# V on ScalarE's DMA queue, K and the weights on SyncE's, in a decode attention kernel

## The chip, the cores and the metric

The kernel runs on one core of a Trainium2 chip. The time is the device time of one execution in microseconds (us); less is better. The core has five engines with their own programs: TensorE (PE, matrix products; PEld are its weight loads), VectorE (DVE), ScalarE (ACT), GpSimd (POOL) and SyncE (SP). They meet only through semaphores. DMAs are issued from an engine's program into that engine's queue, and 16 DMA engines move the data from HBM into SBUF. In the profile "SPq" and "ACTq" are rows of an engine's sequencer, such as the issue of a DMA.

## What is computed

One decode step of attention over a cache, times a gate from a small MLP. B = 2, D = 512, H = 32 heads of Dh = 128, and 8192 cached positions, all in float32:

```python
x  = A_x                                  # [2, 1, 512]
xn = layernorm(x)
q  = (xn @ wq) split into 32 heads        # [2, 32, 1, 128]
scores = q . k_cache * Dh**-0.5           # k_cache, v_cache: [2, 32, 8192, 128]
o  = softmax(scores) . v_cache
s  = o (heads joined, 4096) @ wo          # [2, 1, 512]
g  = silu(gelu(layernorm(xn) @ w1 + b1) @ w2 + b2)
return x + s * g
```

K and V have 268 MB each, wq and wo 8 MB each.

## The kernel before

The 64 heads (2 batches of 32) are taken in N = 32 pairs. A pair's K is 8.39 MB and fills one big SBUF buffer of 128 partitions with 64 KB each: the lower 64 partitions hold one head, the upper 64 the other, 128 positions a partition. There are three such buffers. KBUF[0] and KBUF[1] take K of even and odd pairs, VB takes V of every pair. K and V of pair n are called K(n) and V(n) here. VB holds w1, w2 and the small operands of the setup before V(0), and wo after the last V that it takes; KBUF[1] holds wq at first; V(31) goes into KBUF[0], in two halves.

Each engine loops over the pairs on its own.

- VectorE, `scores`: waits for K(n), multiplies it by q in place (TENSOR_TENSOR, 128x16384), sums over the head's width (TENSOR_REDUCE into sc), takes the maximum per partition (MX), and, after TensorE has transposed MX, the negative maximum per head (nm).
- TensorE, `softmax(n)`: two dummy matmuls (`unread`, bank<-Q,ident, whose result nobody reads), the transpose of MX (signals p_m), and the spread of nm over the partitions. The first of these last matmuls signals p_k: KBUF of this pair is free. The second signals p_n.
- ScalarE: bias from p_n, two exponentials into PZ (s_pz), then it waits for `weighted`, copies its sums out of PSUM (the COPY o<-bank, signal s_o4), and, after p_t, copies the pair's result into OT (a_ot).
- TensorE, `weighted(n)`: waits for s_pz and for V(n) (d_v), 32 matmuls PZ x V (bank<-big,PZ; each of these fp32 matmuls is two rows in the trace), p_v; then, after s_o4, four matmuls (bank<-mod,o). The first of them signals p_free: VB is free. The last signals p_t.

TensorE's order is softmax(0), then for each pair weighted(n), softmax(n+1), and weighted(31) at the end.

SyncE issues all large loads on one queue. Its loop takes p_k, issues K(n+2), takes p_free, issues V(n+1). `take` waits until a semaphore has a count and takes it off again. So in the queue stand K(1), V(0), K(2), V(1), K(3) and so on. At the end come K(31) in two halves, V(30), V(31) in two halves, and then, after p_free of pair 30, wo in eight pieces. ScalarE issues three small loads at the very start (x, b1 and b2, of 4, 5.4 and 2 KB), while SyncE issues w2's last rows, w1, wq, K(0) and the rest of w2.

After the loop the pieces are joined (Z, OA, rl, "on"), "on" is multiplied by wo, and the gate and x are applied.

All operations are recorded through the helper `op`, so nearly all of them have its line, L51, in the profile; L45 is `take` and L41 `wait`. The groups are told apart by the names of their tiles; "big" is any of the three buffers.

Of the kernel before, what the change touches and what calls it, by code (L numbers as in the profile page):

```python
# [4 lines left out]
AF = mybir.ActivationFunctionType  # L5
# [8 lines left out]
class Program:  # L14
# [24 lines left out]
    def wait(self, eng, *tokens):  # L39
        for name, v in self.need(eng, tokens):  # L40
            self.engines[eng].wait_ge(self.sem(name), v)  # L41

    def take(self, eng, name, v=1):

        self.engines[eng].wait_ge(self.sem(name), v).then_inc(self.sem(name), -v)  # L45

    def op(self, eng, method, *args, waits=(), sig=None, by=1, quiet=False, **kwargs):
        need = self.need(eng, waits)
        for name, v in need[:-1]:
            self.engines[eng].wait_ge(self.sem(name), v)  # L50
        ins = getattr(self.engines[eng], method)(*args, **kwargs)  # L51
        for name, v in need[-1:]:
            ins._wait_ge(self.sem(name), v)
        if quiet:
            return None
        name = sig or "own_" + eng
        by = 16 if method == "dma_start" else by
        ins.then_inc(self.sem(name), by)
        self.counts[name] += by
        return name, self.counts[name]  # L60


def decode_kernel(nc, x, kc, vc, wq, wo, w1, b1, w2, b2, out):
# [5 lines left out]
    U = 2  # L69
    HP = P // U  # L70
    KP = S // HP
    HH = H // U
    N = B * HH
    HG = 512 // DH
    NG = H // HG
    SCALE = float(DH) ** -0.5
# [4 lines left out]
    JW = 512 // DH  # L81
# [14 lines left out]
    op, wait, take = pr.op, pr.wait, pr.take  # L96

    def sb(shape, name):
        return nc.alloc_sbuf_tensor(name, list(shape), F32).ap()
# [5 lines left out]
    vf = vc.rearrange("b h s d -> (b h s d)").rearrange("(n p j d) -> n p j d", p=P, j=KP, d=DH)  # L105
# [3 lines left out]
    KBUF, VB = rows[:2], rows[2]  # L109
    used = [0]  # L110

    def boot(p, n):
        a = used[0]
        used[0] += n
        assert used[0] <= KP * DH
        return big[2][:p, a:a + n]
# [10 lines left out]
    sel = boot(P, P)  # L127
# [22 lines left out]
    th = sb([P, P], "th")  # L150
# [5 lines left out]
    SC = [sb([P, KP], f"sc{i}") for i in range(2)]  # L156
    MX = sb([P, 1], "MX")
    nm = sb([1, U], "nm")
    bias = sb([P, 1], "bias")
    RS = sb([P, N], "RS")  # L160
    PZ = sb([P, NT, U, JW], "PZ")
    o4 = sb([P, JW * DH], "o4")
    OT = sb([P, BH], "OT")
# [7 lines left out]
    po = bank[0]  # L171
    pm = bank[1]
    pn = bank[2]
    pt = bank[3]
# [13 lines left out]
    PE_EVENTS = ["xnT", "yT", "ph", "phT", "pq", "pqa"] + [f"pb{g}" for g in range(N // NPB)] + ["pg", "pgate"]  # L188

    def pe(name):  # L190
        return "pe_setup", PE_EVENTS.index(name) + 1

    def pe_n(name, n):
        return name, n + 1

    t = {}
# [9 lines left out]
    def load_k(n, *waits):  # L206
        sems, cuts = ([f"d_k{n % U}", "d_kl"], HALVES) if n == N - 1 else ([f"d_k{n % U}"], (0, KP))
        for name, (c0, c1) in zip(sems, zip(cuts, cuts[1:])):
            op("SP", "dma_start", KBUF[n % U][:, c0:c1], kf[n][:, c0:c1], sig=name, waits=waits)
# [17 lines left out]
    for k in (7, 6, 1, 2, 4, 0):  # L227
# [13 lines left out]
                  op=ALU.add)  # L241
# [59 lines left out]
                     waits=[t["x4m"]])  # L301


    wait("SP", t["sel"], t["qnat"], pe(PE_EVENTS[-1]))
    op("SP", "dma_start", VB, vf[0], sig="d_v")
    kp, vp = (a.rearrange("(i u) p j d -> i u p j d", u=U) for a in (kf, vf))
    with nc.sync.Fori(0, N // U - 2) as i:
        for u in range(U):
            take("SP", "p_k")
            op("SP", "dma_start", KBUF[u], kp[i + 1, u], sig=f"d_k{u}")  # L310
            take("SP", "p_free")
            op("SP", "dma_start", VB, vp[i, 1] if not u else vp[i + 1, 0], sig="d_v")
    for n in range(N - 2 * U, N - 2):
        take("SP", "p_k")
        load_k(n + 2)
        take("SP", "p_free")
        op("SP", "dma_start", VB, vf[n + 1], sig="d_v")
    take("SP", "p_k")
    for i, (c0, c1) in enumerate(zip(HALVES, HALVES[1:])):
        op("SP", "dma_start", KBUF[N % U][:, c0:c1], vf[N - 1][:, c0:c1], sig=f"d_v31{i}")  # L320
    take("SP", "p_free")
    wo_v = wo.rearrange("(p c) n -> p c n", p=P)
    for i, (c0, c1) in enumerate(zip(WO_CUTS, WO_CUTS[1:])):
        for h, (n0, n1) in enumerate(zip(LAST_COLS, LAST_COLS[1:]) if c1 == OC else [(0, D)]):
# [23 lines left out]
    scores(1, Q[:, N - 1, :], ["d_k1", "d_kl"], HALVES)  # L348


    with nc.scalar.Fori(0, N // U) as i:
        for u in range(U):
            take("ACT", "p_n")
            op("ACT", "copy", bias, pn[:, :1], sig="s_b")
            take("ACT", "s_b")
            sc = SC[u].rearrange("p (t j) -> p t j", j=JW)
            for s in range(U):
                r = slice(HP * s, HP * (s + 1))
                op("ACT", "activation", PZ[r, :, s, :], sc[r], AF.Exp, bias=bias[r], scale=SCALE,
                   accum_out=RS.rearrange("p (i u) -> p i u", u=U)[r, i, u:u + 1], sig="s_pz", quiet=s < U - 1)  # L360
            take("ACT", "p_v")
            op("ACT", "copy", o4, po, sig="s_o4")
            take("ACT", "p_t")
            op("ACT", "copy", OT.rearrange("p (i u s) -> p i u s", u=U, s=U)[:, i, u, :], pt[:, :U], sig="a_ot")
    t["OT"] = "a_ot", N

    t["gate"] = op("DVE", "scalar_tensor_tensor", gate, th, 1.0, z, op0=ALU.add, op1=ALU.mult,
# [9 lines left out]
                 op=ALU.mult, waits=[t["rl"], t["on0"], pe_n("p_oa", 0)])  # L377
# [33 lines left out]
    for c in range(ND):  # L411
# [4 lines left out]
        j, k = NF % QT, NF // QT  # L416
# [6 lines left out]
    j, k = NF % QT, NF // QT  # L423
    mm(ph[R * j:R * j + B, k * P:k * P + FT], ones[:1, :B], b1_sb[:, NF * P:], start=False, stop=True, sig="ph")
    by_tile = ident.rearrange("p (j r) -> p j r", r=R)
    for k in range(NH):
        n = min(QT, NF + 1 - k * QT)
# [16 lines left out]
    for g in range(N // NPB):  # L444
        mm(PB[g % len(PB)], sides, QN[:, g * NPB:(g + 1) * NPB, :].rearrange("h n d -> h (n d)"),
           waits=[t["side"], t["QN rest" if g else "QN first"]] + ([t[f"Q{QH}"]] if g >= len(PB) else []),
           sig=f"pb{g}")
    for f in range(NF + 1):
        j = f % QT
# [4 lines left out]
    for j in range(QT):  # L454
        mm(pgate[R * j:R * j + MB, :], mod_b[:, :MB], g_nat[:, j * P:(j + 1) * P], waits=[t["g"], t["mod_b"]],
           sig="pgate" if j == QT - 1 else None)
# [64 lines left out]
    for b in range(B):  # L521
        h = slice(b * H, (b + 1) * H)
        mm(OA[:, b, :OC], Z[:, h].rearrange("p h r -> p (h r)"), mod, waits=[t["Z"]],
           sig="p_oa" if b == B - 1 else None)
    unread(1)
    for i, (c0, c1) in enumerate(zip(WO_CUTS, WO_CUTS[1:])):
        for c in range(c0, c1):
            after = [t["on"], t["mem"], (f"d_wo{i}", 16)]
            if c < WIDE:
                j = c % QT  # L530
# [39 lines left out]
```

## Time and profile before

| what | value |
|---|---|
| median of 3 runs | 1300.62 us (1300.08 to 1300.69) |
| the profiled execution | 1299.61 us |
| its span in the trace | 1298.3 us |
| busy: VectorE, TensorE, ScalarE | 1135.7, 460.9, 72.0 us |
| read from HBM | 559.30 MB, 431 GB/s over the span |
| SyncE's queue (q1) | 559.30 MB, its packets 99.7% of the span of 16 DMA engines |
| ScalarE's queue (q10) | 8 packets, 0.01 MB |

The span is the stretch that the profiler recorded; the execution's own time lies 1.3 us above it. In the queue rows the share is the time that a queue's packets took, of 16 DMA engines over the span. A timeline row gives the start and the duration in us, the engine, the operation, output<-input and how many instructions were merged; in brackets stands how long the engine idled ahead of it. An issue row of a DMA ends long before the data has landed; the landing times are listed apart, as the median from issue to landing.

### The profile page before, as it was taken

The page shows a single profiled execution, that of the slowest core. Times are in us where ns is not written, and L with a number is a line of the kernel's source. Part 1 is how long each engine was busy: PE and PEld are TensorE (multiplying, and loading weights), DVE is VectorE, ACT ScalarE, POOL GpSimd, SP SyncE. Part 2 cuts the span into 40 slices and gives each one's busy share as a digit, 9 for nine tenths or more (in the row PEclk, how much of TensorE's full clock was granted, in tenths as well). Part 3 has the DMA queues.
Part 4 walks back from the last instruction along what each step waited for, and adds up shares of the span by engine and source line. Part 5 has one row for each costly group of instructions (what it writes and reads, how often), then busy time and mean ns, then how long its engine had stood idle before and what let it go on. Part 6 is the DMA issues. An engine that isn't in the chain of part 4 may idle for free. (4 is left out here: it accounts for less than half of the span.)

```text
span 1298.3 us, 7389 instructions
## 1 busy us (share of the span) xinstructions
PE 460.9 (35%) x2958; PEld 148.7 (11%) x2958; DVE 1135.7 (87%) x171; ACT 72.0 (6%) x245; POOL 2.1 (0%) x14
## 2 busy tenths in 40 slices
PE   3813433322433322343322334322334321343337
PEld 1201111001111000111100111100111100111103
DVE  2599999988889988889988888988888988888991
ACT  1100000000000000000000000000000000000000
POOL 0000000000000000000000000000000000000000
PEclk8756776567677556777656777656776666677659
DMA  9999999999999999999999999999999999999998
GB/s 410 436 428 442 430 432 432 428 444 428 438 430 428 440 428 444 428 434 430 428 444 428 440 430 426 440 428 444 428 434 430 430 442 428 440 430 430 423 436 361
DMA packets 11242, 559.39 MB, mean 431 GB/s; under 512 B 1264, under 2 KB 1536, under 8 KB 1892
## 3 DMA queue, kind: packets, MB, share of 16 engines
q1 hardware_dynamic: 11228, 559.30, 99.7%
q8 instruction: 4, 0.07, 0.0%
q10 hardware_dynamic: 8, 0.01, 0.0%
q14 instruction: 2, 0.02, 0.0%
HBM read 559.30 MB, written 0.00 MB: 431 GB/s over the span
## 5 line engine op out<-in xcount | busy, mean ns | idle before, releaser
L51 DVE TENSOR_TENSOR big<-big,Q 128x16384 f32<-128x16384 f32 (+1 forms) x33 | 551.3, 16707 | 73.2 <-DVEq L45 73.2
L51 DVE TENSOR_REDUCE sc<-big 128x128 f32<-128x16384 f32 (+1 forms) x33 | 551.2, 16703 | 4.8
L51 PE MATMUL bank<-big,PZ 128*8 128x512 f32 x2048 | 291.1, 732 | 628.9 <-PEq L45 628.9
L51 PEld LDWEIGHTS bank<-big,PZ 128*8 128x8 f32 x2048 | 60.1, 103 | 832.6 <-issue 832.6
L51 PE MATMUL bank<-Q,ident 128*128 128x512 f32 (+2 forms) x198 | 78.5, 506 | 0.2 <-issue 0.2
L51 ACT COPY o<-bank 128x512 f32<-128x512 f32 x33 | 19.4, 586 | 891.6 <-ACTq L45 880.0
L51 PE MATMUL bank<-ident,MX 128*1 128x128 f32 x32 | 9.3, 291 | 137.9 <-PEq L45 137.8
L51 PE MATMUL bank<-mod,o 128*128 128x2 f32 x256 | 32.8, 250 | 27.4 <-PEq L45 27.4
L51 PEld LDWEIGHTS bank<-mod,o 128*128 128x128 f32 x256 | 31.0, 191 | 55.4 <-issue 55.4
L51 PEld LDWEIGHTS bank<-Q,ident 128*128 128x128 f32 x198 | 33.6, 198 | 16.5 <-issue 16.5
L51 ACT ACTIVATE PZ<-sc,bias 64x128 f32<-64x128 f32 x64 | 25.5, 399 | 6.6 <-ACTq L45 6.2
L51 DVE TENSOR_REDUCE nm<-bank 1x2 f32<-1x128 f32 x32 | 8.9, 279 | 18.9 <-DVEq L45 18.9
L51 DVE TENSOR_TENSOR big<-big,mine 64x512 f32<-64x512 f32 (+1 forms) x2 | 4.5, 2279 | 21.6 <-ACT big L51 21.6
L51 PEld LDWEIGHTS bank<-ident,MX 128*1 128x1 f32 x32 | 2.5, 79 | 162.9 <-issue 162.9
L51 ACT COPY bias<-bank 128x1 f32<-128x1 f32 x32 | 5.1, 159 | 225.2 <-ACTq L45 225.2
L51 PE MATMUL bank<-nm,srow 1*64 1x1 f32 x128 | 10.4, 219 | 10.0 <-PEq L45 9.4
L51 PE MATMUL bank<-big,sides 64*128 64x512 f32 x16 | 12.6, 958 | 3.7 <-DVE big L51 3.7
L51 DVE TENSOR_REDUCE MX<-sc 128x1 f32<-128x128 f32 x32 | 9.2, 286 | 4.7
L51 PE MATMUL bank<-big,xnT 128*2 128x512 f32 x64 | 9.3, 748 | 10.3 <-DMA big<-in_A_wq_dram 10.3
L51 ACT ACTIVATION_READ_ACCUMULATOR PZ<-sc,bias x64 | 11.8, 184 | 0.0
L51 DVE SCALAR_TENSOR_TENSOR res<-bank,gate 128x128 f32<-128x128 f32 x1 | 0.3, 292 | 12.1 <-PE bank L51 12.1
L51 PEld LDWEIGHTS bank<-nm,srow 1*64 1x64 f32 x128 | 8.6, 165 | 16.2 <-issue 16.2
(78 smaller groups left out, 74.8 us busy)
## 6 DMA issues: line engine op xcount, KB each, us to landing
big<-in_A_k_cache_dram SPq DMA_DIRECT2D x2, 4096.0 KB, 35.9
big<-in_A_v_cache_dram SPq DMA_DIRECT2D x2, 4096.0 KB, 35.9
big<-in_B_w_dram SPq DMA_DIRECT2D x1, 2752.0 KB, 10.2
big<-in_B_w_dram SPq DMA_DIRECT2D x1, 2560.0 KB, 52.1
big<-in_A_wo_dram SPq DMA_DIRECT2D x1, 2560.0 KB, 14.7
big<-in_A_wo_dram SPq DMA_DIRECT2D x1, 2048.0 KB, 19.3
big<-in_A_wo_dram SPq DMA_DIRECT2D x1, 1536.0 KB, 22.5
big<-in_A_wo_dram SPq DMA_DIRECT2D x1, 1024.0 KB, 24.5
```

The source lines that it names most:

```text
L51: ins = getattr(self.engines[eng], method)(*args, **kwargs)
```

## The change

V(0) to V(30) are issued by ScalarE into ScalarE's queue. V(0) is issued after th, the last operation of ScalarE's setup. In the loop over the pairs, ScalarE takes p_free behind the copy o<-bank, issues V(n+1), and goes on to p_t and OT. SyncE's loop keeps K alone. V(31) stays on SyncE's queue, and wo there waits for a_ot of pair 30 where it took p_free before. ScalarE's last two pairs stand outside of its loop, without a load.

```diff
-    wait("SP", t["sel"], t["qnat"], pe(PE_EVENTS[-1]))
-    op("SP", "dma_start", VB, vf[0], sig="d_v")
     kp, vp = (a.rearrange("(i u) p j d -> i u p j d", u=U) for a in (kf, vf))
     with nc.sync.Fori(0, N // U - 2) as i:
         for u in range(U):
             take("SP", "p_k")
             op("SP", "dma_start", KBUF[u], kp[i + 1, u], sig=f"d_k{u}")
-            take("SP", "p_free")
-            op("SP", "dma_start", VB, vp[i, 1] if not u else vp[i + 1, 0], sig="d_v")
     for n in range(N - 2 * U, N - 2):
         take("SP", "p_k")
         load_k(n + 2)
-        take("SP", "p_free")
-        op("SP", "dma_start", VB, vf[n + 1], sig="d_v")
     take("SP", "p_k")
...
-    take("SP", "p_free")
+    wait("SP", ("a_ot", N - 1))
...
-    with nc.scalar.Fori(0, N // U) as i:
+    wait("ACT", t["sel"], t["th"])
+    op("ACT", "dma_start", VB, vf[0], sig="d_v")
+
+    def weights(u, i, following):
+        take("ACT", "p_n")
...
+        take("ACT", "p_v")
+        op("ACT", "copy", o4, po, sig="s_o4")
+        if following is not None:
+            take("ACT", "p_free")
+            op("ACT", "dma_start", VB, following, sig="d_v")
+        take("ACT", "p_t")
+        op("ACT", "copy", OT.rearrange("p (i u s) -> p i u s", u=U, s=U)[:, i, u, :], pt[:, :U], sig="a_ot")
+
+    with nc.scalar.Fori(0, N // U - 1) as i:
         for u in range(U):
...
+            weights(u, i, vp[i, 1] if not u else vp[i + 1, 0])
+    for u in range(U):
+        weights(u, N // U - 1, None)
```

SyncE's loop, two pairs, before (the row "ISA" is a `take`; in brackets is the semaphore that it waits for):

```order
L51 ISA [waits p_k]
L51 DMA big<-in_A_k_cache_dram 128x16384
L51 ISA [waits p_free]
L51 DMA big<-in_A_v_cache_dram 128x16384
L51 ISA [waits p_k]
L51 DMA big<-in_A_k_cache_dram 128x16384
L51 DMA big<-in_A_v_cache_dram 128x16384 [waits p_free]
```

The same engine from the loop's first row to the first piece of wo, in the changed kernel:

```order
L51 ISA [waits p_k]
L51 DMA big<-in_A_k_cache_dram 128x16384
L51 ISA [waits p_k]
L51 DMA big<-in_A_k_cache_dram 128x16384
L305 REGISTER_ALU
L305 COMPARE_AND_BRANCH
L51 DMA big<-in_A_k_cache_dram 128x16384 [waits p_k]
L51 DMA big<-in_A_k_cache_dram 128x8192 [waits p_k]
L51 DMA big<-in_A_k_cache_dram 128x8192
L51 DMA big<-in_A_v_cache_dram 128x8192 [waits p_k]
L51 DMA big<-in_A_v_cache_dram 128x8192
L51 DMA big<-in_A_wo_dram 128x5120 [waits a_ot]
```

V has left the loop with its wait; of V only the two halves of V(31) are still there.

ScalarE's loop, the first of its two pairs, before:

```order
L51 COPY bias<-bank 128x1 [waits p_n]
L51 ISA [waits s_b]
L51 ACTIVATE PZ,RS<-sc,bias 64x32x4
L51 ISA
L51 ACTIVATE PZ,RS<-sc,bias 64x32x4
L51 COPY o<-bank 128x512 [waits p_v]
L51 ISA [waits p_t]
L51 COPY OT<-bank 128x2
```

And in the changed kernel:

```order
L51 COPY bias<-bank 128x1 [waits p_n]
L51 ISA [waits s_b]
L51 ACTIVATE PZ,RS<-sc,bias 64x32x4
L51 ISA
L51 ACTIVATE PZ,RS<-sc,bias 64x32x4
L51 COPY o<-bank 128x512 [waits p_v]
L51 ISA [waits p_free]
L51 DMA big<-in_A_v_cache_dram 128x16384
L51 ISA [waits p_t]
L51 COPY OT<-bank 128x2
```

The wait for p_free and the issue of the next V stand between the two copies; the rest is in the order of before.

More of the change, by code (lines that the diff above doesn't have):

```diff
@@ L348, in decode_kernel @@
     scores(1, Q[:, N - 1, :], ["d_k1", "d_kl"], HALVES)
-    with nc.scalar.Fori(0, N // U) as i:
-        for u in range(U):
[L353 to L364, printed above, removed]
+    wait("ACT", t["sel"], t["th"])
+    op("ACT", "dma_start", VB, vf[0], sig="d_v")
+    def weights(u, i, following):
+        take("ACT", "p_n")
+        op("ACT", "copy", bias, pn[:, :1], sig="s_b")
+        take("ACT", "s_b")
+        sc = SC[u].rearrange("p (t j) -> p t j", j=JW)
+        for s in range(U):
+            r = slice(HP * s, HP * (s + 1))
+            op("ACT", "activation", PZ[r, :, s, :], sc[r], AF.Exp, bias=bias[r], scale=SCALE,
+               accum_out=RS.rearrange("p (i u) -> p i u", u=U)[r, i, u:u + 1], sig="s_pz", quiet=s < U - 1)
+        take("ACT", "p_v")
[6 more added lines that the diff above has]
+    with nc.scalar.Fori(0, N // U - 1) as i:
+        for u in range(U):
+            weights(u, i, vp[i, 1] if not u else vp[i + 1, 0])
+    for u in range(U):
+        weights(u, N // U - 1, None)
     t["OT"] = "a_ot", N
```

## The prediction

> **What bounds the kernel now.** I read the page's DMA rows first, then the order of events within one pair on the timeline, then the landing times. The page's 40 slices and its queue table:
>
> ```profile
> span 1298.3 us, 7389 instructions
> DMA  9999999999999999999999999999999999999998
> q1 hardware_dynamic: 11228, 559.30, 99.7%
> L51 DVE TENSOR_TENSOR big<-big,Q 128x16384 f32<-128x16384 f32 (+1 forms) x33 | 551.3, 16707 | 73.2 <-DVEq L45 73.2
> ```
>
> All traffic that counts is on one queue (q1, SyncE's), and its packets fill the 16 DMA engines for 99.7% of the span. VectorE, the busiest engine, stalls 73.2 us for K. The kernel is bound by DMA. One pair of the steady part, in order of time:
>
> ```profile
> 608.57 0.33 SPq L51 DMA_DIRECT2D big<-in_A_v_cache_dram  x1
> 615.49 0.33 SPq L51 DMA_DIRECT2D big<-in_A_k_cache_dram  x1
> 617.68 17.23 DVE L51 TENSOR_TENSOR big<-big,Q 128x16384 f32<-128x16384 f32 x1 [2.83 <-DVEq L45]
> 635.05 17.22 DVE L51 TENSOR_REDUCE sc<-big 128x128 f32<-128x16384 f32 x1
> 636.93 8.37 PE L51 MATMUL bank<-big,PZ 128*8 128x512 f32 x64 [21.66 <-PEq L45]
> 645.45 0.59 ACT L51 COPY o<-bank 128x512 f32<-128x512 f32 x1 [28.71 <-ACTq L45]
> 646.78 0.33 SPq L51 DMA_DIRECT2D big<-in_A_v_cache_dram  x1
> 647.07 1.96 PE L51 MATMUL bank<-Q,ident 128*128 128x512 f32 x4
> 647.40 0.16 ACT L51 COPY OT<-bank 128x2 f32 x1 [1.36 <-ACTq L45]
> 652.85 0.27 PE L51 MATMUL bank<-ident,MX 128*1 128x128 f32 x1 [3.81 <-PEq L45]
> 654.27 0.33 SPq L51 DMA_DIRECT2D big<-in_A_k_cache_dram  x1
> 656.38 17.23 DVE L51 TENSOR_TENSOR big<-big,Q 128x16384 f32<-128x16384 f32 x1 [2.83 <-DVEq L45]
> ```
>
> The period is 656.38 - 617.68 = 38.70 us for one K and one V, 8.39 MB each, so a transfer alone takes 19.35 us. V has one buffer. From V's landing (TensorE starts at 636.93) to the issue of the next V (646.78) nothing can move for V. That gap is free now, because the K issued at 615.49 is still in the queue. The landing times of the two kinds, and the rate and packets of 200 us:
>
> ```profile
> big<-in_A_k_cache_dram SPq DMA_DIRECT2D x31, 40.6
> big<-in_A_v_cache_dram SPq DMA_DIRECT2D x31, 28.1
> ```
>
> ```profile
> DMA packets 1503, 86.97 MB, mean 435 GB/s; under 512 B 176, under 2 KB 176, under 8 KB 176
> ```
>
> 1503 - 176 completions = 1327 data packets in 200 us on 16 engines: 2.41 us each, 64 KB, one partition's row; 128 rows over 16 engines are 8 packets per engine and transfer. K waits 40.6 - 19.35 us behind V, and V 28.1 - 19.35 us behind K: one transfer is always in service and one queued, each served whole.
>
> **The change.** It adds no bytes and no compute. 31 V issues go from SyncE's program to ScalarE's, each an issue row of 0.33 us. ScalarE's copies at 645.45 and 647.40 leave room for it; what is queued behind the wait on p_free there is the OT copy, which is needed only at the end. Price: none; were it late, OT would slip by 0.3 us in every pair and still cost 0.3 us once. SyncE now waits for p_k alone. K isn't issued sooner for that, since softmax follows weighted on TensorE, whichever engine issues V. What changes is the service: K and V now stand in two queues. Does a transfer on one queue wait for the backlog of the other? The only place with two busy queues is the start:
>
> ```profile
> 0.74 0.88 SPq L51 DMA_DIRECT2D big<-in_B_w_dram  x2
> 1.32 0.53 ACTq L51 DMA_DIRECT2D big<-in_B_b_dram  x2
> big<-in_B_w_dram SPq DMA_DIRECT2D x1, 2752.0 KB, 10.2
> ```
>
> w1 (2752 KB, 22 KB a row, so 8 rows per engine and 0.81 us a row at 435 GB/s) is issued on SyncE's queue by 1.62 and lands about 11.4 us into the span. b2 (one packet of 2 KB and its completion) is issued on ScalarE's queue by 1.85, after w1. The queue rows of 4.5 to 4.7, of 5.4 to 5.6 and of 5.5 to 11.5 us:
>
> ```profile
> q10 hardware_dynamic: 1, 0.00, 2.6%
> ```
>
> ```profile
> q10 hardware_dynamic: 1, 0.00, 0.3%
> ```
>
> ```profile
> q1 hardware_dynamic: 109, 2.74, 106.6%
> ```
>
> b2's data goes at 4.5 to 4.7 and its completion at 5.4 to 5.6; in the last stretch its queue (q10) is gone and SyncE's moves 2.74 MB more. So ScalarE's queue isn't served behind SyncE's backlog: it gets in between the rows of one transfer, and between its data and its completion some 0.8 us pass, the time of one 22 KB row. I take the engines to alternate, row by row, between two queues that both have work.
>
> The Trainium skill, page "DMA: Bandwidth & Descriptors", section "Queues, rings and completion order", says that each engine goes round robin over the queue rows and switches only after a whole packet, typically 9 to 17 descriptors. If the 8 rows and the completion of a transfer were one such packet, V would go through whole as before and the sum would be 1300 us; b2 cutting into w1's 8 rows speaks against that reading, and for alternation by rows.
>
> With alternation the free gap is paid for. Take V(n) landed at time 0, steady state:
> - to the issue of V(n+1): 9.85 here; 106.22 - 95.11 = 11.11 and 1266.90 - 1256.26 = 10.64 by the rows below; mean 10.5, and 0.15 from landing (608.57 + 28.2) to TensorE's start: 10.7 us;
> - issue and landing of a transfer that has no queue ahead of it: 0.33 for the issue row and 1.1 for the 4 KB output below: 1.4 us;
> - K(n+3) is issued when softmax(n+1) is through. VectorE has finished scores(n+1) long before, so this follows the dummy matmuls (end 647.07 + 1.96 = 649.03) by 654.27 - 652.85 = 1.42: 650.45, or 3.7 us after V's issue. In that time V gets 1.5 rows, so two before the first K row; then 6 of V and 6 of K in turn: 14 rows, and as with b2 one K row more before V's completion: 15 x 2.42 = 36.3 us.
>
> Sum 10.7 + 1.4 + 36.3 = 48.4 us a pair instead of 38.7: +9.7. K(n+3) lands right after, and the engines then stand idle for about 9 us of each pair. VectorE needs 34.5 us for scores and a few for softmax, and is covered by 48.4. Bounds: halves without rows, 3.7 + 2 x (19.35 - 3.7) = 35.0, give 47.1; no wait of the completion, 14 rows, 46.0; K issued before V's first row is through, 16 rows, 50.8. I take the 48.4, since b2 is the nearest row.
>
> The start, by its rows:
>
> ```profile
> 40.31 0.33 SPq L51 DMA_DIRECT2D big<-in_A_k_cache_dram  x1
> DMA to landing us min/median/max: 35.3/35.3/35.3
> 66.30 0.31 ACT L51 ACTIVATE th<-z 128x128 f32<-128x128 f32 x1
> 86.34 17.23 DVE L51 TENSOR_TENSOR big<-big,Q 128x16384 f32<-128x16384 f32 x1
> 87.12 0.36 SPq L51 DMA_DIRECT2D big<-in_A_k_cache_dram  x1
> 95.11 9.62 PE L51 MATMUL bank<-big,PZ 128*8 128x512 f32 x64 [8.21 <-PEq L45]
> 106.22 0.34 SPq L51 DMA_DIRECT2D big<-in_A_v_cache_dram  x1
> 123.03 0.33 SPq L51 DMA_DIRECT2D big<-in_A_k_cache_dram  x1
> 144.25 0.33 SPq L51 DMA_DIRECT2D big<-in_A_v_cache_dram  x1
> ```
>
> V0 starts at 67.7 (behind th, 66.61) and shares with K1, which had 7.9 us left (it lands at 75.6): K1 slips to about 84, before its use at 86.34. V0 has then 3.4 rows, 5 when K2 starts at 88; 3 rows in turn and the completion are 7 x 2.42, so V0 lands at 105 instead of 95. V1 starts at 116.7, has 3 rows when K3 starts at 124, and lands after 11 rows more at 151. V2 starts at 162.7 and takes the full 36.3: 199.4, where before it landed at 144.25 + 28.1 = 172.4: +27. From V2 to V30 are 28 periods: 28 x 9.7 = 272. V30 lands 299 us later than before.
>
> The end:
>
> ```profile
> 1256.26 9.31 PE L51 MATMUL bank<-big,PZ 128*8 128x512 f32 x64 [21.75 <-PEq L45]
> 1266.90 3.65 SPq L51 DMA_DIRECT2D big<-in_A_wo_dram  x8
> 1283.51 0.23 DVE L51 TENSOR_TENSOR on<-bank,rl 128x64 f32<-128x64 f32 x1 [0.72 <-PE bank L51]
> 1296.53 0.63 SPq L51 DMA_DIRECT2D out_dram<-res  x1
> SPq L41 <- DMA out_dram<-res: 1.1, 1, 1.1
> L51 PE MATMUL bank<-big,on 128*17 128x512 f32 (+1 forms) x88 | 9.3, 485 | 2.6 <-DMA big<-in_A_wo_dram 2.5
> ```
>
> V31 follows K31 on SyncE's queue, in the place of a next K. wo now waits for the OT copy, 0.8 us after the old point (647.56 against 646.78), but has the engines alone: 10.7 + 0.8 + 1.4 + 19.4 = 32 us after V30's landing the last of it is there. TensorE then sets the end: "on" is ready 1283.7 - 1256.3 = 27.4 us after that landing, wo's matmuls take 9.3, and from the issue of the output to the end (1296.53 + 0.63 + 1.1) go 1.7 with some 0.8 of VectorE ahead of it: 39 us instead of the 42 from 1256.3 to 1298.3. So the end moves by 299 - 3 = 296: a span of 1594 us. The profiled execution lasted 1299.61 us with a span of 1298.3; 1.3 on top gives 1595. Its time lies 1.0 us under the median of the runs, 1300.62, which I leave as noise.
>
> **Rivals.** First: the two queues are served in the order of issue, or V gets over two thirds of the engines. V's share s decides: 10.7 + 1.4 + 3.7 + 15.65/s = 38.7 at s = 0.69. Above it K's stream fills the gap as now, and the time stays at 1300 us. For it speaks that a whole transfer is served before the next in one queue; against it b2. The whole-packet reading of the Trainium skill's page "DMA: Bandwidth & Descriptors", above, would be this case.
>
> Second: K comes first whenever it has work. V then gets 3.7 us, waits 19.35 for K and takes the remaining 15.65: 38.7 + 12.1 = 50.8 a pair, 2.4 x 28 = 67 us more: 1662. Nothing in the rows prefers one queue.
>
> Third, faster: two queues feed the engines better than one. The best stretches of the page's rate line show 444 GB/s where the mean is 431, and at 444 the 559 MB take 1260 us. It needs the first rival's share as well; against it are rows that stand back to back at 2.41 us already.
>
> **How the numbers follow.** Alternation 0.83; order of issue or V favoured 0.09; K favoured 0.04; better fed 0.04. Likeliest: 1595. Its bounds of 46.0 to 50.8 a pair are 28 x -2.4 and 28 x +2.4, 1528 to 1662; I put the lower end at 1470 for a V share between a half and 0.69 (44 us a pair), and the upper at 1650, inside K's case. That holds 0.8. Slower by over 0.2% (what a measurement of this kernel can tell from none): 0.87; within: 0.09; faster: 0.04.
>
> **What would show it.** In the profile after: two hardware queues, of 260 MB (31 V) and 299 MB; DMA digits of 7 to 9 instead of 9 and a mean near 350 GB/s; V landing some 37 us after its issue, K about as long; VectorE's starts 48 us apart; TensorE's weighted matmuls waiting for V while VectorE waits for softmax, no longer for K. If V lands in 20 us, the share is not equal and the sum falls.

## The result, and the profile after

The changed kernel takes 1567.05 us in the median of 6 runs (1563.66 to 1574.0), the kernel before 1300.64. The ratio is 1.205, with a 95% interval of 1.2035 to 1.2073. The profiled execution of the changed kernel lasted 1563.66 us with a span of 1562.4.

The page's span, 40 slices and queues, after:

```profile
span 1562.4 us, 7398 instructions
DMA  9999997878988778877889777897778977879798
q1 hardware_dynamic: 6764, 299.25, 44.4%
q10 hardware_dynamic: 4472, 260.06, 39.7%
```

The same bytes as before now stand in two queues, and the DMA engines, full before, have holes from the seventh slice on. Where they are is seen in one pair on the timeline:

```profile
630.56 0.34 ACTq L51 DMA_DIRECT2D big<-in_A_v_cache_dram  x1
633.32 17.23 DVE L51 TENSOR_TENSOR big<-big,Q 128x16384 f32<-128x16384 f32 x1
633.99 48.03 SPq L51 DMA_DIRECT2D big<-in_A_k_cache_dram  x2
650.69 17.22 DVE L51 TENSOR_REDUCE sc<-big 128x128 f32<-128x16384 f32 x1
667.06 9.73 PE L51 MATMUL bank<-big,PZ 128*8 128x512 f32 x64 [33.27 <-PEq L45]
668.05 0.29 DVE L51 TENSOR_REDUCE MX<-sc 128x1 f32<-128x128 f32 x1
676.94 0.58 ACT L51 COPY o<-bank 128x512 f32<-128x512 f32 x1 [41.69 <-ACTq L45]
678.26 0.34 ACTq L51 DMA_DIRECT2D big<-in_A_v_cache_dram  x1
680.78 0.28 DVE L51 TENSOR_REDUCE nm<-bank 1x2 f32<-1x128 f32 x1 [12.44 <-DVEq L45]
```

(The SPq row merges two issues of K, at 633.99 and 681.68.) V is issued at 630.56, K 3.4 us later. V lands 36.4 us after its issue, where it took 28.1. TensorE starts at 667.06, and the next V is issued at 678.26. VectorE is through with its scores at 668 and waits 12.44 us for softmax, which stands behind weighted on TensorE. Over the whole run that wait of nm is 353.0 us (18.9 before), and the wait for K is 8.5 us (73.2 before): K is no longer what is late. The two groups (the last number is the idle time ahead of them):

```profile
L51 DVE TENSOR_TENSOR big<-big,Q 128x16384 f32<-128x16384 f32 (+1 forms) x33 | 551.3, 16707 | 8.5 <-DVEq L45 8.4
L51 DVE TENSOR_REDUCE nm<-bank 1x2 f32<-1x128 f32 x32 | 8.9, 279 | 353.0 <-DVEq L45 353.0
```

The landing of V over the run, the packets that start between 631 and 639.2 us, and three stretches by windows, whose last two columns are the DMA share and the GB/s:

```profile
big<-in_A_v_cache_dram ACTq DMA_DIRECT2D x31, 36.4
```

```profile
DMA packets 48, 3.15 MB, mean 384 GB/s; under 512 B 0, under 2 KB 0, under 8 KB 0
```

```profile
637.00:666.00 29.00, 0.00 (x0) 0.00 (x0) 28.85 (x2) 0.00 (x0) 0.00 (x0) 0.52 1.01 438
672.00:679.00 7.00, 6.12 (x53) 2.19 (x46) 0.00 (x0) 0.69 (x2) 0.00 (x0) 0.96 0.00 0
400.00:1200.00 800.00, 203.90 (x1328) 65.36 (x1328) 584.32 (x66) 30.18 (x112) 0.00 (x0) 0.63 0.82 350
```

The 48 packets of 64 KB are all on ScalarE's queue: three rows of V on each of 16 engines ahead of K's first. While both queues have work (637 to 666) the engines move 438 GB/s, as much as with one queue: nothing is lost by sharing. How they share, by the two queues' packets that start between 639.6 and 666.1 us:

```profile
q1 hardware_dynamic: 94, 6.16, 53.6%
q10 hardware_dynamic: 86, 5.24, 45.7%
```

K has 94 rows there (q1). V has its last 80 rows, five on each engine, and 6 of the small packets with which a load reports its completion (q10). Cut into stretches of 5 us from 640 to 660, each has 16 rows of V and 16 or 17 of K: one row of each per engine and turn. The windows of a microsecond show the end of the load as well: V's 16 last rows start between 661 and 662, 16 rows of K between 663 and 665, and V's 16 completions only between 665 and 667.

From 672 to 679, while TensorE works on V, the engines move nothing. K landed 4.8 us behind V (633.99 + 37.8), and the next V can't be issued yet. Over 800 us the engines are busy 0.82 of the time.

### The profile page after: what moved, and what is told of

Same layout as the page of the kernel before. It is cut to its first block, busy times and chain, and to the rows that moved or that the text cites. A ratio compares the mean times of both kernels' runs of the same rounds, so it can differ in the third digit from the quotient of the medians.

```text
span 1562.4 us, 7398 instructions
## 1 busy us (share of the span) xinstructions
PE 454.4 (29%) x2958; PEld 149.5 (10%) x2958; DVE 1135.2 (73%) x171; ACT 72.0 (5%) x245; POOL 2.1 (0%) x14
## 3 DMA queue, kind: packets, MB, share of 16 engines
q1 hardware_dynamic: 6764, 299.25, 44.4%
## 5 line engine op out<-in xcount | busy, mean ns | idle before, releaser
L51 DVE TENSOR_REDUCE nm<-bank 1x2 f32<-1x128 f32 x32 | 8.9, 279 | 353.0 <-DVEq L45 353.0
L51 PE MATMUL bank<-nm,srow 1*64 1x1 f32 x128 | 9.2, 199 | 11.2 <-PEq L45 11.0
L51 ACT ACTIVATION_READ_ACCUMULATOR PZ<-sc,bias (+1 forms) x64 | 11.8, 185 | 0.0
L51 PE MATMUL bank<-big,on 128*17 128x512 f32 (+1 forms) x88 | 7.3, 477 | 0.1
L51 ACT COPY OT<-bank 128x2 f32 (+1 forms) x32 | 5.1, 160 | 43.6 <-ACTq L45 43.6
```

## Experiments

Times are medians beside the kernel before on the same chip, which took 1299.67 to 1300.04 us there. The theory: the DMA engines take a row of one queue and a row of the other in turn, so V, which has one buffer, takes nearly two transfers' time, and its idle gap between landing and next issue is no longer covered. The rivals: two busy queues cost by themselves, whatever their rows; ScalarE is a bad place to issue from; the late wo or the first V costs. The diffs are shortened, and stand against the changed kernel.

**One queue, but ScalarE's.** K(2) to K(31), V and wo are all issued by ScalarE in the old order.

```diff
+        if load_next_k is not None:        # was SyncE's
+            take("ACT", "p_k")
+            load_next_k()
         take("ACT", "p_v")
         op("ACT", "copy", o4, po, sig="s_o4")
...
```

> K(2) to K(31), V and wo all on ScalarE's queue, issued by ScalarE's loop over the pairs in the order of the kernel before (K(n+2) behind the exponentials, V(n+1) behind the copy of the sums, wo where it was); SyncE issues only the setup and K(0), K(1). Theory (what costs is that two queues are busy at once): one queue serves in order, 1300 to 1306 us. Rival (ScalarE is a bad place to issue from, or its queue is slower): 1567 us or more.

1300.01 us, ratio 1.000 (0.999 to 1.0009). ScalarE's issue and ScalarE's queue cost nothing; by this run what costs is that two queues are busy together.

**K with short rows.** K in 4 DMAs, each a quarter of the columns:

```diff
-            op("SP", "dma_start", KBUF[u], kp[i + 1, u], sig=f"d_k{u}")
+            for c in range(0, KP, KP // 4):
+                op("SP", "dma_start", KBUF[u][:, c:c + KP // 4], kp[i + 1, u][:, c:c + KP // 4], sig=f"d_k{u}")
```

> The changed kernel, with every K load cut into 4 DMAs of a quarter of the columns, so rows of 16 KB instead of 64; V keeps rows of 64 KB on ScalarE's queue. Theory (the DMA engines alternate between the two queues row by row): V gets four bytes for each of K, so a V load takes about 7.3 us with three rows ahead of K's first, 5 x (2.42 + 0.6) = 15 in turn, 1 to 2 of latency: 24 to 25 us from issue instead of 36.4. 10.9 + 24.5 = 35 us is under the 38.7 of the bytes, so the DMA engines are full again and the time is 1295 to 1312 us. Rival (two busy queues cost the same whatever the rows, by halves of the bytes or by a lower rate): 1567 us as before. Rival (ScalarE is a slow issuer): 1567 us.

1355.16 us, ratio 1.0408 (1.0381 to 1.0435): 212 of the 267 us are back, though every DMA stands in the same queue as in the changed kernel. V's landing and 800 us of the steady part:

```profile
big<-in_A_v_cache_dram ACTq DMA_DIRECT2D x31, 28.6
```

```profile
400.00:1200.00 800.00, 263.03 (x1660) 86.22 (x1660) 698.98 (x81) 37.71 (x140) 0.00 (x0) 0.66 0.99 419
```

The engines are full again (0.99). V lands 28.6 us after its issue instead of the 24.5 I expected. K now always has rows queued, so no V row goes ahead alone: eight turns of 3.0 us are 24.2. And V's first row comes late: behind the V issue at 624.72, all 49 packets that start between 625 and 627 us are K's, and V's first rows start between 627 and 631. So V isn't the bound; the bytes are, at 419 GB/s and 40.0 us a pair (8.39 MB twice). The time missed its range by 43 us: 1.3 us a pair are lost to the lower rate, and the start and the end cost the rest. At the start V(0) now pushes K(1) aside: VectorE starts on pair 1 at 95.96 instead of 86.34.

```profile
95.96 17.22 DVE L51 TENSOR_TENSOR big<-big,Q 128x16384 f32<-128x16384 f32 x1 [9.07 <-DVEq L45]
```

**K with short rows on one queue.** The kernel before with the same K in quarters:

> The kernel before, everything on SyncE's queue, with K in 4 DMAs and rows of 16 KB. It tells what of the 55 us that the two-queue kernel with K in quarters still lacks is owed to short rows, and what to two queues. If short rows cost by themselves (0.611 us each for a quarter of 2.42, and the mean 0.632): between 32 x 0.007 = 0.2 and 32 x 0.03 = 0.9 us a pair, 1307 to 1330 us. If it is the meeting of two queues: 1300 to 1306.

1307.37 us, ratio 1.0055 (1.0038 to 1.0072), and the same 800 us:

```profile
400.00:1200.00 800.00, 269.38 (x1736) 85.53 (x1736) 721.42 (x82) 38.45 (x142) 0.00 (x0) 0.67 1.00 431
```

Short rows alone cost 7 us (431 GB/s against the 434 of whole rows). The other 12 GB/s of the two-queue kernel with quarters come only where short rows and a second queue meet. Why was not followed up.

**K with half rows** (the same edit with 2 DMAs):

> K in 2 DMAs, rows of 32 KB against V's 64 KB. Turns by rows: V's load is 1 + 3.2 + 2 x 2.42 + 5 x 3.63 + 1.21 + 0.45 = 28.9 us (36.4 with K whole), the pair 10.9 + 28.9 = 39.8 us, just over the 38.7 to 39.5 that the bytes need: 1310 to 1340 us, at or under the kernel with quarters (1355), whose engines were busy all the time and which pays for its short rows. If V's share had to be four to one to cover the gap, it would lie between 1355 and 1567.

1365.68 us, ratio 1.0508 (1.0477 to 1.0538), over the range. V's landing is 30.2 us in the median, one half row (1.2 us) more than the sum, and the pair 41.0 us, so V's gap still binds by a little and the engines stay at 0.96. The sum was one half row short, and "at or under the kernel with quarters" was wrong by 10 us. That half the K row is nearly enough, and a share of four to one isn't needed, holds.

**V with short rows,** the mirror image:

```diff
-            op("ACT", "dma_start", VB, following, sig="d_v")
+            for c in range(0, KP, KP // 4):
+                op("ACT", "dma_start", VB[:, c:c + KP // 4], following[:, c:c + KP // 4], sig="d_v")
```

> The mirror image: V in 4 DMAs with rows of 16 KB, K whole with rows of 64 KB. Alternation by rows: V is now the disfavoured one: after some 4.6 us alone its remaining 24 quarter rows go 8 in turn with K's 8 rows (8 x 3.03 = 24.2 us) and 16 alone (9.7 us), 39.5 us a load where 36.4 are measured, +3 us a pair: 1640 to 1670 us. Halves by bytes: 1567 us or a little less.

1698.23 us, ratio 1.306: slower still, as only the theory of turns has it, and beyond the range. V(3)'s first DMA and V(29)'s are issued at

```profile
226.75 1.93 ACTq L51 DMA_DIRECT2D big<-in_A_v_cache_dram  x4
1564.11 1.93 ACTq L51 DMA_DIRECT2D big<-in_A_v_cache_dram  x4
```

26 pairs apart: 51.4 us a pair, the 51.3 of the sum (48.3 and 3). V(3) is 29 us later than in the changed kernel; from V(29)'s issue to the end of the span are 131.7 us, 22 more than there. I had only counted the steady pairs.

**Both with short rows:**

> Both in quarters: rows of 16 KB in both queues. Alternation by rows gives halves again, only without the graininess of 64 KB: 1 + 4.6 alone + 29.5 in turn + 0.6 = 35.7 us a V load, under a us less a pair: 1540 to 1570 us. If it were smaller DMAs as such that help, this would be as fast as the kernel with K alone in quarters, near 1300 us.

1571.58 us, ratio 1.2085. By its issues of V(3) (199.05) and V(29) (1441.24) the pair takes 47.8 us. The gain of 0.5 us a pair is there, and the end gives it back (128.1 us from V(29)'s issue to the end of the span, 109.5 in the changed kernel); the total is 2 us over the range. Short DMAs as such help nothing: the ratio of the row sizes does.

**V issued earlier.** V goes out at p_v, ahead of the copy of the sums:

```diff
         take("ACT", "p_v")
-        op("ACT", "copy", o4, po, sig="s_o4")
         if following is not None:
-            take("ACT", "p_free")
             op("ACT", "dma_start", VB, following, sig="d_v")
+        op("ACT", "copy", o4, po, sig="s_o4")
```

> ScalarE issues the next V as soon as the weighted sum is through (p_v), ahead of the copy of the sums, in place of after p_free. V's idle gap gets 1.45 us shorter and K comes 1.8 us later behind V. Theory (the pair lasts as long as V's gap and V's load in turn with K): 1.45 us less a pair if still three V rows go ahead of K's first, 46.8 us and 1525 us; 3.9 less if it becomes four, 44.4 us and 1460 us; so 1455 to 1530. By halves of the bytes without rows: 3.25 less, 1476. Rival (V's idle gap doesn't bound the pair): 1567.

1459.35 us, ratio 1.123 (1.115 to 1.130). From the end of V's matmuls to the issue of the next V it is 0.28 us (600.71 to 600.98) where the changed kernel has 1.48 (629.08 to 630.56): the issue moved by 1.2 us, not by the 1.45 expected, and is worth 108 us. The pair takes 44.4 us ((1264.8 - 199.3) / 24), as expected for a fourth row.

**V issued later,** behind the OT copy:

```diff
-        if following is not None:
-            take("ACT", "p_free")
-            op("ACT", "dma_start", VB, following, sig="d_v")
         take("ACT", "p_t")
         op("ACT", "copy", OT...[:, i, u, :], pt[:, :U], sig="a_ot")
+        if following is not None:
+            take("ACT", "p_free")
+            op("ACT", "dma_start", VB, following, sig="d_v")
```

> ScalarE issues the next V behind the OT copy instead of ahead of it: V's issue comes 1.0 us later, K's stays. Turns by rows: the gap is 1.0 us longer, and K arrives while V's first row is in service instead of its second, so two V rows go ahead instead of three and V's load takes one K row more, 2.4 us: 3.4 a pair, 1655 to 1670 us. By halves without rows: 2.0 a pair, 1623. If V's gap isn't what bounds the pair: 1567.

1647.07 us, ratio 1.267 (1.259 to 1.276): 80 us for some 0.9 us (2.34 from the end of V's matmuls, 615.29, to V's issue, 617.63), 8 under the range, and well over the 1623 of equal halves. The pair takes 51.2 us ((1283.3 - 208.7) / 21, by the issues of V(3) and V(24)), 2.9 more and not the 3.4 expected. The landing is only 1.3 us later in the mean, since in the changed kernel 12 of the 26 V loads of that stretch took 38.6 us or more already; V's matmuls took 9.9 us instead of 9.2, which the sum had left out. The landing of V after its issue, for V's DMAs between 190 and 1300 to 1440 us, in the kernel with the early issue, the changed kernel and the one with the late issue:

```profile
DMA to landing us min/median/max: 33.8/34.0/36.5
```

```profile
DMA to landing us min/median/max: 36.3/36.5/38.8
```

```profile
DMA to landing us min/median/max: 38.6/38.8/39.0
```

The steps are 2.4 us, one 64 KB row, and the landing goes by the slowest of the 16 engines. In the kernel with the early issue the packets that start between 601 and 611.9 us, behind V's issue at 600.98, show the fourth row:

```profile
DMA packets 64, 4.19 MB, mean 385 GB/s; under 512 B 0, under 2 KB 0, under 8 KB 0
```

All 64 are V's, four rows on each engine. In the kernel with the late issue, the three rounds behind the V issue at 617.63 (618 to 626.3 us) are:

```profile
q10 hardware_dynamic: 40, 2.62, 79.1%
q1 hardware_dynamic: 8, 0.52, 14.6%
```

So K comes in after two rows of V on 8 of the 16 engines, and after three on the others.

**The queues exchanged.** K(2) to K(31) on ScalarE's queue, V on SyncE's:

> The mirror image of the change: K(2) to K(31) and V(31) on ScalarE's queue (issued at p_k, ahead of the bias copy), V(0) to V(30) and wo on SyncE's. Turns by rows know no preferred queue: 1545 to 1590 us. If SyncE's queue were preferred, V would get through sooner, 1300 us; if ScalarE's were, over 1600.

1559.53 us, ratio 1.1999 (1.195 to 1.204). Neither queue is preferred: by the expectation a preference would have given 1300 us or over 1600.

**The small parts alone.** The kernel before, with V(0) issued by ScalarE behind th, and wo behind the OT copy:

> The kernel before with only the change's small parts: V(0) issued by ScalarE behind th, and wo behind the OT copy of pair 30; V(1) to V(31) and K stay on SyncE's queue. All theories: the two queues meet once, for K(1) and V(0), and wo's issue is 0.8 us later behind a full queue: 1298 to 1304 us. If the late wo or the meeting of V(0) and K(1) mattered, some 5 to 10 us more.

1301.41 us, ratio 1.001 (0.9999 to 1.002). They cost nothing that shows.

**Both remedies,** K in halves and V at p_v:

> Two queues, K in halves (32 KB rows), and V issued at p_v: the two remedies together. V's load 30.2 us with K in halves, less 1.2 for one K row that falls behind a fourth V row, and the gap shorter by 1.45: 10.9 - 1.45 + 29.0 = 38.4 us, under the 38.7 that the bytes need. By turns the engines are then full nearly all the time: 39 to 39.7 us a pair, 1308 to 1335 us. It isn't expected to beat the kernel before. If the two remedies don't add: 1355 to 1366.

1323.62 us, ratio 1.0178 (1.016 to 1.0196). The engines are at 0.99 and 425 GB/s. With a larger share for V and a shorter gap the two queues come within 24 us of one queue; none of the versions beat it.

## Why the prediction came out

The step on which all else stood was right: the engines alternate by rows between two busy queues, and V's gap, covered before, is paid for in each pair. The predicted pair was 48.4 us. The issues of V(3) and V(29),

```profile
197.36 0.34 ACTq L51 DMA_DIRECT2D big<-in_A_v_cache_dram  x1
1452.89 0.34 ACTq L51 DMA_DIRECT2D big<-in_A_v_cache_dram  x1
```

give (1452.89 - 197.36) / 26 = 48.3. Term by term:

- Issue and service were put at 1.4 + 36.3 = 37.7. Of the 26 landings of V(3) to V(28), 14 lie at 36.3 to 36.5 us and 12 at 38.6 to 38.8, 37.5 in the mean. That leaves 48.3 - 37.5 = 10.8 for the gap from landing to issue, which was put at 10.7 (in the pair shown it is 678.26 - 667.06 = 11.2 from TensorE's start).
- The prediction let two rows of V go ahead of K. In the 36.4 us loads three go ahead on every engine. In the load issued at 678.26, which lands after 38.6, the third round (684 to 686.3 us) is 15 rows of V and one of K: one engine of the 16 had only two rows ahead, and that sets the landing. By the prediction's rule three rows ahead are 35.3 us and two 37.7; both kinds of load take about 1.1 us more than that. So the agreement within 0.1 us a pair is partly luck: a head start that was too short for half of the loads and a service that was 1.1 us too quick cancel.
- The completion of V, which I took to wait for one more K row after b2's model, does so: the microsecond windows above have a row of K between V's last row and V's completion on every engine. The sum needs it too: three rows ahead and five turns of 4.84 us without that wait are 31.5 us, and with the 1.4 and it they are 35.3.
- Some 9 us of idle engines a pair were forecast: 0.18 of 48.3 is 8.7.
- VectorE waits for softmax and not for K, ScalarE's copies and the issue cost nothing, the small parts of start and end nothing: as forecast, the last two by runs of their own.

The Trainium skill's page "DMA: Bandwidth & Descriptors", section "Queues, rings and completion order", has the engines go round robin over the queues, and the trace agrees: 16 rows of V and 16 or 17 of K in each 5 us. Its packet of typically 9 to 17 descriptors is not the unit in which these loads alternate: one row per engine and turn, and landings in steps of one row, speak for single rows of 64 KB.

The total is 28 us under the 1595 of the prediction. Its sum was off in two terms, by the profiled spans 1594 and 1562.4:

- **The start.** V(2) was to land at 199.4; TensorE starts on it at 186.52, 13 us earlier. K(1) was kept in the queue until about 84, and V(0) was given 105; it was there at 100.01. V(1) was then issued 11.6 us ahead of K(3) (111.46 and 123.08) and V(2) 6.9 us ahead of K(4) (152.60 and 159.49), where the sum had 7.3 and 3.7, so both had more rows alone. (Two slips in the prediction's arithmetic change nothing: 162.7 + 36.3 are 199.0 and not 199.4, and V's share at which the pair stays at 38.7 comes out at 0.68, not 0.69.)
- **The end.** V(29) and V(30) share the engines with K(31) and V(31), which are loaded in halves, with rows of 32 KB. By the rule of the prediction itself a V row of 64 KB then waits for half as much. It was stated that K(31) and V(31) come in halves, and the sum used 28 equal periods all the same. Landings of V(29) and V(30) after their issue:

```profile
DMA to landing us min/median/max: 31.1/31.1/31.1
DMA to landing us min/median/max: 30.1/30.1/30.1
```

From V(29)'s issue to V(30)'s are 41.8 us, and V(30) lands 6.3 us sooner than the median: some 13 us in all. Start and end make 26 of the 31.6 us; 26 pairs by 0.1 and the tail behind V(30) (1562.4 - 1524.97 = 37.4 instead of 39) nearly all of the rest.

The rivals are out by runs: service in the order of issue would have left 1300 us; a preference for a queue doesn't go with the exchanged queues at 1559.53; a preference for K, which the exchange alone would not rule out, doesn't go with equal turns in the trace and would have taken 1662; and a better feed by two queues isn't there, at 438 GB/s with both busy and 434 with one.

## What to carry to other kernels

A queue that is always full hides the time in which a single buffer can't be refilled, because the next transfer is already behind it. Split over two queues with rows of one size, the buffer's transfer took nearly twice as long here (36.4 to 38.8 us against 19.35 alone), and the gap came out in every round. Before moving a stream to a queue of its own, look for the buffer that has no second copy, and add to its gap a load at half rate: gap + 2 x load less the head start, against the period now. If two queues must be used, the runs here speak for longer rows in the stream with the single buffer, and for issuing it ahead of the other.

## What had not been expected

- A head start of a microsecond decides whole rows: V issued 1.2 us earlier gained 108 us, 0.9 us later lost 80. K's first row starts over 5 us after its issue (633.99, and no packet of K before 639.2), while a V issued when the engines are idle starts about 1 us after its issue (630.56, first rows from 631.4). So a queue that gets work beside a busy one waited for more than the row in service; why was not followed up.
- The share of a queue goes by the size of its rows: with K at 64, 32 and 16 KB rows against V's 64 KB the kernel takes 1567, 1366 and 1355 us, and with V at 16 KB against K's 64, 1698.
- K in rows of 16 KB gave 431 against 434 GB/s in one queue, but 419 beside a second queue.
